# Moving the second pair's K copies, the first V, the weight steps and three squares in an attention and two gated layers

## The chip, the cores and the metric

The kernel runs on one core of a Trainium2 chip. The metric is the device time of one execution in microseconds (us). TensorE (PE) does matrix products and transposes into eight banks of PSUM; VectorE (DVE), ScalarE (ACT) and GpSimd (POOL) do the element work, and GpSimd works on SBUF only; SyncE (SP) issues all transfers. Each engine takes its instructions in the order of the program and waits by semaphores.

## The reference

Three stages, in float32:

```
q_pool = mean of each two rows of q                       (2, 8, 576, 64)
scores = q_pool @ k^T / 8 ; attn = softmax(scores)        (2, 8, 576, 1152)
x = attn @ v, heads side by side                          (1152, 512)
x = rms-normed x * rms_g ; g = x @ w_gate (512 x 1536)
x = (g * sigmoid(g) * (x @ w_val)) @ w_out                (1152, 512)
out = (sigmoid(x @ w_gate2) * (x @ w_val2)) @ w_out2      (1152, 512)
```

The weights come in as words of 64 bits, and the kernel makes float32 of them.

## The kernel before

For precision every operand of a product is split into a high part, rounded to a shorter float, and a low part, the rest; a product is two or three matrix products. The split costs two instructions: one writes the high part (ScalarE, or GpSimd at line 145), one subtracts it (VectorE, or GpSimd at line 146).

**Units of work.** The 16 heads are done in 8 pairs. A pair's scores are 576 query rows in five blocks of 128 rows (`QCOL`; the block c = 0 has half of each head) by three units of 384 keys (`SU`). A *score unit* (`s_unit`, line 476) is two products into one bank (line 505), which VectorE moves out with its maximum (line 509); after three units VectorE reduces the maxima to `nb` (line 511) and ScalarE takes the exponential (line 522). `t_unit` (line 532) transposes the exponentials into a bank (lines 544 and 555) and splits them into `et`: ScalarE writes the high part (line 567) and VectorE the low one (line 568), or ScalarE copies the bank to `er` (line 563) and GpSimd splits it. `av_unit` multiplies with V (line 582). One head takes 18 slots, one transpose unit in each.

**Order.** `at(g, rank, fn)` puts a step into slot g; `run_agenda` calls the steps by slot, then by rank, and each engine gets its instructions in that order. A pair's score units begin 15 slots ahead of its first transposes (`AHEAD`), so the first pair's units are in slots -15 to 19 and the second pair's from slot 21.

**Banks.** PSUM's eight banks have three tags: "s" has two for scores, "t" four for transposes, "o" two for outputs. The first pair's score units use "s" and "o" in turns of two (line 497). The early weight step `w_a1(True)` writes its result to a bank of "t" (line 212).

**Queues.** All transfers are on SyncE's queue, in program order. A transfer that waits holds up all that stand behind it. K, Q and V of a pair are loaded ahead (`load_pair`, `load_v`); a K or Q tile is loaded again only after its reader is through.

**Second pair.** `prep_pair` transposes Q (two groups) and K (three groups) of a pair in the slots `PREP_SECOND`, has GpSimd split them, and then copies the parts on SyncE's queue to where the score products read them: Q in `qq`, K's high part `kh` and low part `kl` into `kk`, in slots `PREP_SECOND_MOVES` (lines 471 to 474). The first score unit of a pair reads the keys 0 to 383, the second 384 to 767. K comes over in a copy of 512 columns and one of 640.

**Weights.** `w_spread` puts five steps of one weight block into the slots `W_SLOTS` of the odd heads 3, 5, 7, 9 and 11: `w_a1` (ScalarE, line 213), `w_b1` and `w_b2` (VectorE, lines 231 and 235), `w_a2` (ScalarE, line 220), `w_b3` (GpSimd, line 241).

**First batch's x.** When the first four pairs are done, `x_steps` takes squares on ScalarE (line 647), roots, norms on GpSimd (line 658) and transposes on TensorE (line 663), in slots counted back from the end of attention, 288 (`X_SQUARES`, `X_TURNS`).

After attention, TensorE does the layers' products (lines 736, 839, 868) while the other engines prepare weights and results.

Of the kernel before, what the change touches and what calls it, by code (L numbers as in the profile page):

```python
# [8 lines left out]
F32 = mybir.dt.float32  # L9
F32R = mybir.dt.float32r  # L10
U32 = mybir.dt.uint32
AF = mybir.ActivationFunctionType
ALU = mybir.AluOpType
# [3 lines left out]
P = 128  # L17
# [15 lines left out]

PREP = (0, 3, 3, 7, 9)
PREP_MOVES = (4, 8, 12, 12)
PREP_SECOND = (3, 6, 7, 11, 12)
PREP_SECOND_MOVES = (11, 12, 14, 14)

PREP_V, POOL_Q, LOAD = 13, 11, 13


FIRST_SUMS, FIRST_Q, SECOND_SUMS, FIRST_V, POOL_Q_SECOND = -1, 3, 4, 7, 11
SECOND_GROUPS = ((6, 3, True, 0), (11, 5, False, 0), (8, 3, True, 1), (11, 3, True, 2), (14, 5, False, 1))
SECOND_DVE = ((False, 1), (True, 0), (True, 2))

W_SLOTS, W_SPLIT = (2, 3, 4, 6, 9), 16
W_WORDS, W_EARLY = 5, 4


X_SQUARES = ((-101, -89, -81), (-54, -59))
X_ROOTS = (-40, -35)
X_NORMS = ((-14, -27, -25), (-20, -17))
X_TURNS = ((-6, -20, -17), (-13, -10))
X_LAST = ((4, 5, 6), (9, 12))

UP_SLOTS = (1, 3, 5, 7)
# [5 lines left out]
def tile_attention_moe_moe(ctx, tc, q, k, v, w_gate1, w_val1, w_out1, rms_g, w_gate2, w_val2, w_out2, out):  # L64
# [3 lines left out]
    nc = tc.nc  # L68
    B, H, S, D = q.shape
# [3 lines left out]
    NK = S // P  # L73
# [21 lines left out]
    def pool(name, side="left", **kw):  # L95
        p = tc.alloc_tile_pool(name=name, bufs=1, side=side, **kw)
        pools.append(p)
        return p
# [9 lines left out]
    ap = pool("ap")  # L108
# [5 lines left out]
    def bank(tag, name):  # L114
        return ps.tile([P, 512], F32, tag=tag, bufs=NBANK[tag], name=name)
# [15 lines left out]
    def at(g, rank, fn):  # L131
        count[0] += 1
        agenda.setdefault(g, []).append((rank, count[0], fn))
# [9 lines left out]
    def split(hi, lo, x):  # L143

        nc.gpsimd.tensor_scalar(hi, x, 1.0, 1.0, op0=ALU.mult, op1=ALU.mult)
        nc.gpsimd.tensor_tensor(lo, x, hi.bitcast(F32), op=ALU.subtract)
# [148 lines left out]
    kk, qq, vv, esb, osb, tbank = {}, {}, {}, {}, {}, {}  # L295
    raw, rcp, xall, sums, both_sums, eneg, oacc, kst = {}, {}, {}, {}, {}, {}, {}, {}
# [20 lines left out]
    def load_v(i):  # L317
        raw["v", i] = ap.tile([P, NK, D], F32, tag="vraw", bufs=1, name="vraw")
        nc.sync.dma_start(raw["v", i], v[i // H, i % H].rearrange("(p c) d -> p c d", c=NK))

    def pool_q(p):
        kr, qr = raw[p]
        qs = ap.tile([P, NQC, P], F32, tag="qsum", bufs=1, name="qsum")
        qd = qs.rearrange("p c (j d) -> p j c d", j=2)
        nc.gpsimd.tensor_tensor(qd, qr[:, :, :, 0:D], qr[:, :, :, D:2 * D], op=ALU.add)
        raw[p] = (kr, qs)

    def prep_v(i):
        vv[i] = ap.tile([P, NK, P], F32R, tag="vv", bufs=2, name="vv")
        split(vv[i][:, :, 0:D], vv[i][:, :, D:P], raw.pop(("v", i)))  # L330
        if i + 1 < NHEAD:
            load_v(i + 1)

    def k_transposes(p, g):
        n = min(4, NK - 4 * g)
        t = bank("t", "kT")
        for c in range(n):
            nc.tensor.transpose(t[:, c * P:(c + 1) * P], raw[p][0][:, 4 * g + c, :], ident)  # L338
        return t[:, 0:n * P], slice(4 * g * P, (4 * g + n) * P)
# [22 lines left out]
    def prep_first():  # L362
# [56 lines left out]
        def head1(g0, is_k, g):  # L419
# [3 lines left out]
            at(g0, 13, lambda: nc.scalar.activation(hi, t, AF.Copy, scale=sc))  # L423
            if (is_k, g) in SECOND_DVE:
                at(g0 + 1, 19, lambda: nc.vector.scalar_tensor_tensor(lo, t, sc, hi.bitcast(F32), op0=ALU.mult, op1=ALU.subtract))
# [25 lines left out]
    def prep_pair(g0, p):  # L451
# [15 lines left out]

        slots, moves = (PREP_SECOND, PREP_SECOND_MOVES) if p == 1 else (PREP, PREP_MOVES)
        for sl, (is_k, g) in zip(slots, ((False, 0), (False, 1), (True, 0), (True, 1), (True, 2))):
# [6 lines left out]
    def s_unit(g, p, k):  # L476

        n, u = divmod(k, NSU)  # L480
        j, c = SCORES[p][n]
        i = 2 * p + j
        both = c == 0 and p > 0
        if k == 0:
            both_sums[p] = ap.tile([P, 2, NQC], F32, tag="sums", bufs=2, name="sums")
            for h in (i, i + 1):
                sums[h] = both_sums[p][:, h - i]
                esb[h] = {}
        if u == 0:
            e = ap.tile([P, NSU * SU], F32, tag="e", bufs=8, name="e")  # L490
            esb[i][c] = e, 0
            if both:
                esb[i + 1][c] = e, 1
            eneg[i, c] = (ap.tile([P, NSU], F32, tag="m", bufs=3, name="m"), ap.tile([P, 1], F32, tag="nb", bufs=3, name="nb"))
        e, _ = esb[i][c]
        m, nb = eneg[i, c]
        s = bank("s" if p or k % 4 < 2 else "o", "s")
        kc = slice(u * SU, (u + 1) * SU)
        if both:
            kh, kl = kst[p]  # L500
            products = ((qbd[:, 0], kh), (qbd[:, 0], kl), (qbd[:, 1], kh))
        else:
            products = [(qq[i][:, part, QCOL[c]:QCOL[c] + P], kk[i]) for part in range(2)]
        for n1, (qs, ks) in enumerate(products):
            nc.tensor.matmul(s[:, 0:SU], qs, ks[:, kc], start=(n1 == 0), stop=(n1 == len(products) - 1))  # L505

        def top():

            nc.vector.tensor_scalar(e[:, kc], s[:, 0:SU], 1.0, None, op0=ALU.mult, op1=ALU.max, accum_out=m[:, u:u + 1])  # L509
            if u == NSU - 1:  # L510
                nc.vector.tensor_reduce(nb, m, op=ALU.max, axis=AX.X, negate=True)

        def swap():
            for h in range(2):
                nc.gpsimd.tensor_copy(sums[i + 1][h * QH:(h + 1) * QH, 0:1], sums[i][(1 - h) * QH:(2 - h) * QH, 0:1])

        def add_small():
            nc.gpsimd.tensor_scalar(both_sums[p], both_sums[p], 1e-9, 1.0, op0=ALU.add, op1=ALU.mult)

        at(g, 17, top)  # L520
        if u == NSU - 1:
            at(g + EXP_LAG, 12, lambda: nc.scalar.activation(e, e, AF.Exp, bias=nb, scale=1.0, accum_out=sums[i][:, c:c + 1]))  # L522
            if both:
                at(g + 4, 24, swap)
            if n == len(SCORES[p]) - 1:
                at(g + 4, 25, add_small)
# [104 lines left out]
    def x_steps(g, b, part):  # L631
# [52 lines left out]
        else:  # L684
            sq = [max(g, END + x) for x in X_SQUARES[part]]
            rt = END + X_ROOTS[part]
            nm = [END + x for x in X_NORMS[part]]
            tt = [END + x for x in X_TURNS[part]]
        for c in range(n):
# [8 lines left out]
    END = NHEAD * NJ  # L698
    S0, S00 = -AHEAD, -AHEAD_FIRST
    prep_first()  # L700
    at(S0 + FIRST_V, 50, lambda: prep_v(0))
    at(S0 + POOL_Q_SECOND, 50, lambda: pool_q(1))
    for p in range(NP):
        for n in range(len(SCORES[p]) * NSU):
            g = 2 * p * NJ + (S0 if p else S00) + n * 2 * NJ // (len(SCORES[p]) * NSU)
            at(g, 2, lambda g=g, p=p, n=n: s_unit(g, p, n))
    for i in range(NHEAD):
        p, odd = divmod(i, 2)
# [205 lines left out]
```

## Time and profile before

| | |
|---|---|
| median of 3 runs | 738.91 us (738.82 to 739.23) |
| profiled execution | 740.92 us, its span 738.7 us |
| TensorE busy | 722.2 us (98% of the span) |
| VectorE, ScalarE, GpSimd busy | 461.0, 432.5, 399.4 us |
| mean granted TensorE clock | 0.993 of full speed |

In rows of a timeline the first number is the start in us from the span's start, the second how long it lasted (of several merged instructions, from the first's start to the last's end); then engine, line, operation, tiles (out<-in), shapes and count; in brackets the idle time of that engine just before and what ended it. "PEld" is TensorE's loading of the operand that stays in the array; it runs beside the products ("PE"), so a pause shows on both with slightly different lengths. "SPq" is SyncE's issuing. A row of the windows view gives a stretch, its length, then the busy us of PE, PEld, DVE, ACT and POOL with their instruction counts, the granted clock (1.00 is 2.4 GHz, 0.50 is 1.2 GHz), the share of the DMA engines that was busy, and GB/s. A row of transfer issues gives out<-in, queue, operation, count, size and the time from issue to landing in us.

### The profile page before, as it was taken

The page shows a single profiled execution, that of the slowest core. Times are in us where ns is not written, and L with a number is a line of the kernel's source. Part 1 is how long each engine was busy: PE and PEld are TensorE (multiplying, and loading weights), DVE is VectorE, ACT ScalarE, POOL GpSimd, SP SyncE. Part 2 cuts the span into 40 slices and gives each one's busy share as a digit, 9 for nine tenths or more (in the row PEclk, how much of TensorE's full clock was granted, in tenths as well). Part 3 has the DMA queues.
Part 4 walks back from the last instruction along what each step waited for, and adds up shares of the span by engine and source line. Part 5 has one row for each costly group of instructions (what it writes and reads, how often), then busy time and mean ns, then how long its engine had stood idle before and what let it go on. Part 6 is the DMA issues. An engine that isn't in the chain of part 4 may idle for free.

```text
span 738.7 us, 12479 instructions
## 1 busy us (share of the span) xinstructions
PE 722.2 (98%) x4501; PEld 692.8 (94%) x4501; DVE 461.0 (62%) x1108; ACT 432.5 (59%) x871; POOL 399.4 (54%) x439
## 2 busy tenths in 40 slices
PE   7969999999999999999999999999999999999997
PEld 6969999999999999999999999999999999998886
DVE  7848988989898887788766754322265455553010
ACT  6748898988899885665544545334255445445000
POOL 5547788888877781466434537443145335437100
PEclk9989999999999999999999999999999999999999
DMA  7443754748365100334223224322032223122011
GB/s 208 103 96 73 175 122 131 163 104 201 74 168 117 46 1 1 115 118 134 89 62 112 87 63 140 92 79 85 29 115 65 78 87 114 58 86 87 0 58 71
DMA packets 69981, 70.30 MB, mean 95 GB/s; under 512 B 19552, under 2 KB 60896, under 8 KB 69920
## 3 DMA queue, kind: packets, MB, share of 16 engines
q1 hardware_dynamic: 69920, 69.51, 33.9%
q8 instruction: 35, 0.57, 0.3%
q14 instruction: 26, 0.21, 0.1%
HBM read 52.69 MB, written 2.36 MB: 75 GB/s over the span
## 4 chain that ended last, share of the span: by engine, by line
PE 93%; DVE 2%; ACT 1%; DMA 1%; SPq 1%; issue 1%; POOL 0%; ACTq 0%; DVEq 0%
PE acc L736 41%; PE s L505 10%; PE acc L839 10%; PE acc L868 10%; PE o L582 10%; PE eT L555 6%; PE eT L544 4%; PE kT L338 1%; PE qT L347 1%; DVE e L509 1%; DVE et L568 1%; DMA kk<-kl 1%; ACT e L522 1%; PE oT L615 1%; PE xT L663 0%
## 5 line engine op out<-in xcount | busy, mean ns | idle before, releaser
L736 PE MATMUL acc<-xh,w 128*128 128x384 f32 (+2 forms) x1184 | 295.8, 331 | 0.0
L736 PEld LDWEIGHTS acc<-xh,w 128*128 128x128 f32 x1184 | 212.0, 188 | 0.0
L736 PE MATMUL acc<-xl,w 128*128 128x384 f32 (+2 forms) x592 | 195.5, 330 | 0.0
L256 POOL TENSOR_TENSOR w<-wr,w 128x512 fp32r<-128x512 f32 x68 | 100.2, 1474 | 160.9 <-ACT w L255 158.5
L509 DVE TENSOR_SCALAR_CACHE_REDUCE e<-s 128x384 f32<-128x384 f32 x219 | 119.3, 551 | 33.0 <-PE s L505 30.4
L582 PE MATMUL o<-et,vv 128*128 128x256 f32 (+1 forms) x576 | 126.2, 327 | 0.2 <-DVE e L509 0.2
L241 POOL TENSOR_TENSOR wr<-wsg,wr 128x512 uint32<-128x512 uint32 x72 | 93.9, 1304 | 44.0 <-DVE wsg L235 44.0
L505 PE MATMUL s<-kk,qq 128*128 128x384 f32 x396 | 108.2, 359 | 9.0 <-DMA kk<-kl 6.2
L736 PEld LDWEIGHTS acc<-xl,w 128*128 128x128 f32 x592 | 111.2, 188 | 0.0
L568 DVE TENSOR_TENSOR et<-eT,et 128x512 fp32r<-128x512 f32 (+1 forms) x173 | 94.7, 554 | 5.4 <-ACT et L567 4.4
L567 ACT ACTIVATE et<-eT 128x512 fp32r<-128x512 f32 (+1 forms) x173 | 83.6, 490 | 23.4 <-PE eT L544 12.1
L747 ACT ACTIVATE sg<-acc 128x384 f32<-128x384 f32 (+2 forms) x74 | 35.4, 481 | 96.1 <-PE acc L736 96.1
L522 ACT ACTIVATE e<-e,nb 128x1152 f32<-128x1152 f32 x73 | 91.3, 1251 | 0.0
L750 DVE TENSOR_TENSOR sg<-acc,sg 128x384 f32<-128x384 f32 (+2 forms) x74 | 40.5, 547 | 80.2 <-PE acc L736 74.4
L582 PEld LDWEIGHTS o<-et,vv 128*128 128x128 f32 x576 | 82.9, 192 | 0.7 <-DVE e L509 0.5
L213 ACT ACTIVATE wg<-wraw 128x512 f32<-128x512 f32 x72 | 48.2, 669 | 52.9 <-DVE wsg L235 32.2
L235 DVE SCALAR_TENSOR_TENSOR wsg<-wg,wsg 128x512 uint32<-128x512 uint32 x72 | 77.1, 1071 | 2.3
L505 PEld LDWEIGHTS s<-kk,qq 128*128 128x128 f32 x396 | 63.6, 192 | 11.8 <-issue 6.4
L839 PE MATMUL acc<-hh,w 128*128 128x384 f32 x288 | 73.3, 334 | 0.0
L231 DVE TENSOR_SCALAR wsg<-wg 128x512 uint32<-128x512 uint32 x72 | 42.6, 592 | 35.1 <-POOL wr L241 35.0
L555 PE MATMUL eT<-ident,e 128*128 128x128 f32 x351 | 61.9, 276 | 1.3 <-ACT er L563 0.6
L544 PE MATMUL eT<-ident,e 128*128 128x128 f32 x288 | 54.0, 275 | 0.0
(113 smaller groups left out, 1085.3 us busy)
## 6 DMA issues: line engine op xcount, KB each, us to landing
wraw<-in_moe_w_gate_dram SPq DMA_DIRECT2D x24, 512.0 KB, 3.5
wraw<-in_moe_w_val_dram SPq DMA_DIRECT2D x24, 512.0 KB, 3.5
wraw<-in_moe_w_out_dram SPq DMA_DIRECT2D x24, 512.0 KB, 3.4
qq<-qq SPq DMA_DIRECT2D x21, 288.0 KB, 3.2
vraw<-in_v_dram SPq DMA_DIRECT2D x16, 288.0 KB, 3.7
kraw<-in_k_dram SPq DMA_DIRECT2D x14, 288.0 KB, 5.1
qraw<-in_q_dram SPq DMA_DIRECT2D x14, 256.0 KB, 4.5
out_dram<-ob SPq DMA_DIRECT2D x9, 256.0 KB, 2.0
```

Source lines behind the costliest of these rows:

```text
L241: nc.gpsimd.tensor_tensor(x["r"], x["s"], x["r"], op=ALU.add)
L256: nc.gpsimd.tensor_tensor(t[:, 1], r, t[:, 0].bitcast(F32), op=ALU.subtract)
L505: nc.tensor.matmul(s[:, 0:SU], qs, ks[:, kc], start=(n1 == 0), stop=(n1 == len(products) - 1))
L509: nc.vector.tensor_scalar(e[:, kc], s[:, 0:SU], 1.0, None, op0=ALU.mult, op1=ALU.max, accum_out=m[:, u:u + 1])
L522: at(g + EXP_LAG, 12, lambda: nc.scalar.activation(e, e, AF.Exp, bias=nb, scale=1.0, accum_out=sums[i][:, c:c + 1]))
L544: nc.tensor.transpose(t[:, o:o + P], esb[i][c][0][:, ks], ident)
L555: nc.tensor.transpose(t[:, o:o + P], e[:, ks], ident if c or half else swap_id)
L567: at(g, 12, lambda: nc.scalar.activation(hi, t, AF.Copy))
L568: at(g + 1, 20, lambda: nc.vector.tensor_tensor(lo, t, hi.bitcast(F32), op=ALU.subtract))
L582: nc.tensor.matmul(o[:, 0:n], vv[i][:, kc, :], et[:, k, x * n:(x + 1) * n], start=(done == 0), stop=(done == 2 * NK - 1))
L736: nc.tensor.matmul(acc[:, 0:nt], wt[:, ws, dc * P:(dc + 1) * P], xs[:, dc], start=(dc == 0 and n == 0), stop=(dc == NDM - 1 and n == 2))
L839: nc.tensor.matmul(acc[t][:, 0:NTT], w[:, ws, (fc % 4) * P:(fc % 4 + 1) * P], hs[fc][:, cs], start=(fc == 0 and n == 0), stop=(fc == NFC - ...
```

## The change

- The second pair's last two K transposes come in slots 10 and 11 (11 and 12 before); Q's copies in slot 10, K's copies in 11, 12 and 12 (12, 14 and 14 before), so ahead of slot 13, where the next V and the third pair are loaded.
- The first V is split in two steps: its high half in slot 10 of the start, its low half in slot 12 (slots counted from -15), where both came in slot 7; the sum of the second pair's Q comes in slot 12 instead of 11.
- The low part of the second head's first K group is made on GpSimd, with a copy by ScalarE, instead of on VectorE.
- The first pair's score units from slot 0 on use only the banks "s".
- The weight steps come in the slots 4, 5, 6, 8, 10 of their heads.
- Two of the first batch's three early squares move from slots 187 and 199 to 210 and 214 (the third stays at 207); two x transposes move one slot later.

```diff
-PREP_SECOND = (3, 6, 7, 11, 12)
-PREP_SECOND_MOVES = (11, 12, 14, 14)
+PREP_SECOND = (3, 6, 7, 10, 11)
+PREP_SECOND_MOVES = (10, 11, 12, 12)
-FIRST_SUMS, FIRST_Q, SECOND_SUMS, FIRST_V, POOL_Q_SECOND = -1, 3, 4, 7, 11
+FIRST_SUMS, FIRST_Q, SECOND_SUMS, FIRST_V, POOL_Q_SECOND = -1, 3, 4, (10, 12), 12
-SECOND_DVE = ((False, 1), (True, 0), (True, 2))
+SECOND_DVE = ((False, 1), (True, 2))
-W_SLOTS, W_SPLIT = (2, 3, 4, 6, 9), 16
+W_SLOTS, W_SPLIT = (4, 5, 6, 8, 10), 16
-X_SQUARES = ((-101, -89, -81), (-54, -59))
+X_SQUARES = ((-78, -74, -81), (-54, -59))
-X_TURNS = ((-6, -20, -17), (-13, -10))
+X_TURNS = ((-6, -20, -17), (-12, -9))
...
+    def first_v(lower):
+        if not lower:
+            vv[0] = ap.tile([P, NK, P], F32R, tag="vv", bufs=2, name="vv")
+            nc.gpsimd.tensor_scalar(vv[0][:, :, 0:D], raw["v", 0], 1.0, 1.0, op0=ALU.mult, op1=ALU.mult)
+            return
+        nc.gpsimd.tensor_tensor(vv[0][:, :, D:P], raw.pop(("v", 0)), vv[0][:, :, 0:D].bitcast(F32), op=ALU.subtract)
+        load_v(1)
...
-        s = bank("s" if p or k % 4 < 2 else "o", "s")
+        s = bank("s" if p or g >= 0 or k % 4 < 2 else "o", "s")
...
-    at(S0 + FIRST_V, 50, lambda: prep_v(0))
-    at(S0 + POOL_Q_SECOND, 50, lambda: pool_q(1))
+    for sl, lower in zip(FIRST_V, (False, True)):
+        at(S0 + sl, 52, lambda lower=lower: first_v(lower))
+    at(S0 + POOL_Q_SECOND, 51, lambda: pool_q(1))
```

What the change does to the order shows at three places. On SyncE's queue, at the second pair's copies (`qq`, `kk` from `kh` and `kl`) and the loads (`vraw`, `qraw`, `kraw`), before:

```order
L358 DMA qq<-qq 64x1152 x3
L358 DMA kk<-kh 64x512
L358 DMA kk<-kl 64x512
L319 DMA vraw<-in_v_dram 128x576
L308 DMA qraw<-in_q_dram 128x4x128 x2
L311 DMA qraw<-in_q_dram 64x2x128 x2
L314 DMA kraw<-in_k_dram 128x9x64 x2
L358 DMA kk<-kh 64x640
L358 DMA kk<-kl 64x640
L358 DMA kk<-kh 64x1152
L358 DMA kk<-kl 64x1152
```

The same place now (the lines are ten further on):

```order
L367 DMA qq<-qq 64x1152 x3
L367 DMA kk<-kh 64x512
L367 DMA kk<-kl 64x512
L367 DMA kk<-kh 64x640
L367 DMA kk<-kl 64x640
L367 DMA kk<-kh 64x1152
L367 DMA kk<-kl 64x1152
L320 DMA vraw<-in_v_dram 128x576
L309 DMA qraw<-in_q_dram 128x4x128 x2
L312 DMA qraw<-in_q_dram 64x2x128 x2
L315 DMA kraw<-in_k_dram 128x9x64 x2
```

Four copies went from behind the seven loads to a place ahead of them.

On GpSimd, in the start (`qsum` from `first`: the second head's Q sum; `kk` and `qq` from `kqt`: low parts of the second head; `vv`: the first V; `qsum` from `qraw`: the second pair's Q sum), before:

```order
L400 TENSOR_TENSOR qsum<-first 128x5x64 x2
L145 TENSOR_SCALAR vv<-vraw 128x9x64
L146 TENSOR_TENSOR vv<-vraw,vv 128x9x64
L429 TENSOR_TENSOR kk<-kqt,kk 64x384
L325 TENSOR_TENSOR qsum<-qraw 128x2x5x64
L429 TENSOR_TENSOR qq<-kqt,qq 128x320
```

And now:

```order
L409 TENSOR_TENSOR qsum<-first 128x5x64 x2
L438 TENSOR_TENSOR kk<-kqt,kk 64x384 x2
L338 TENSOR_SCALAR vv<-vraw 128x9x64
L438 TENSOR_TENSOR qq<-kqt,qq 128x320
L326 TENSOR_TENSOR qsum<-qraw 128x2x5x64
L340 TENSOR_TENSOR vv<-vraw,vv 128x9x64
```

One more low part of K came in, Q's low part went ahead of the Q sum, and V's lower half went behind it.

On VectorE, in an odd head with weight steps (`e,m<-s`: a score unit moved out; `et<-eT`: a low part of transposed exponentials; `wsg`: the weight steps), before:

```order
L592 TENSOR_TENSOR osb<-o,osb 64x256
L231 TENSOR_SCALAR wsg<-wg 128x512
L509 TENSOR_SCALAR e,m<-s 128x384
L568 TENSOR_TENSOR et<-eT,et 128x320
L235 SCALAR_TENSOR_TENSOR wsg<-wg,wsg 128x512
L509 TENSOR_SCALAR e,m<-s 128x384
L511 TENSOR_REDUCE nb<-m 128x1
L568 TENSOR_TENSOR et<-eT,et 128x320
L509 TENSOR_SCALAR e,m<-s 128x384 x2
```

And now:

```order
L601 TENSOR_TENSOR osb<-o,osb 64x256
L518 TENSOR_SCALAR e,m<-s 128x384
L577 TENSOR_TENSOR et<-eT,et 128x320
L518 TENSOR_SCALAR e,m<-s 128x384
L520 TENSOR_REDUCE nb<-m 128x1
L232 TENSOR_SCALAR wsg<-wg 128x512
L577 TENSOR_TENSOR et<-eT,et 128x320
L236 SCALAR_TENSOR_TENSOR wsg<-wg,wsg 128x512
L518 TENSOR_SCALAR e,m<-s 128x384 x2
```

The two weight steps went behind the second of the score units, on both sides of an `et`.

## Rows read from the trace of the kernel before

**Rows 1.** Page, part 1: busy us, share of the span, instructions

```profile
PE 722.2 (98%) x4501; PEld 692.8 (94%) x4501; DVE 461.0 (62%) x1108; ACT 432.5 (59%) x871; POOL 399.4 (54%) x439
```

**Rows 2.** Timeline of PE at the second pair's second score unit

```profile
43.94 0.98 PE L505 MATMUL s<-kk,qq 128*128 128x384 f32 x2 [6.18 <-DMA kk<-kl]
```

**Rows 3.** Timeline of SyncE's queue, 20 to 46 us

```profile
...
30.16 0.73 SPq L358 DMA_DIRECT2D kk<-kl  x1
...
39.28 0.59 SPq L358 DMA_DIRECT2D kk<-kl  x1
...
```

**Rows 4.** Transfer issues, 20 to 50 us: size and time to landing

```profile
...
kk<-kl SPq DMA_DIRECT2D x1, 160.0 KB, 4.5
...
kk<-kl SPq DMA_DIRECT2D x1, 128.0 KB, 3.1
...
```

**Rows 5.** Timeline of POOL: low parts of the second pair's Q and K

```profile
23.56 0.74 POOL L146 TENSOR_TENSOR qq<-kqt,qq 128x256 fp32r<-128x256 f32 x1
...
30.71 0.46 POOL L146 TENSOR_TENSOR kl<-kqt,kh 128x128 fp32r<-128x128 f32 x1
```

**Rows 6.** Windows: three stretches of the first 50 us

```profile
0.00:9.70 9.70, 7.34 (x34) 5.33 (x35) 4.97 (x16) 4.48 (x7) 4.48 (x15) 1.00 0.51 149
...
18.80:22.00 3.20, 3.20 (x15) 3.01 (x14) 1.96 (x9) 2.07 (x4) 1.91 (x4) 0.50 0.02 5
...
43.90:49.20 5.30, 5.26 (x21) 5.06 (x22) 2.18 (x7) 1.31 (x3) 1.55 (x4) 0.50 0.09 24
```

**Rows 7.** Timeline of all engines, 12 to 34 us

```profile
15.33 0.55 DVE L509 TENSOR_SCALAR_CACHE_REDUCE e<-s 128x384 f32<-128x384 f32 x1
...
17.02 0.59 ACT L567 ACTIVATE et<-eT 128x512 fp32r<-128x512 f32 x1
...
17.45 0.19 PEld L505 LDWEIGHTS s<-kk,qq 128*128 128x128 f32 x1 [1.99 <-POOL qq L429]
...
17.65 0.69 DVE L568 TENSOR_TENSOR et<-eT,et 128x512 fp32r<-128x512 f32 x1 [0.29 <-ACT et L567]
...
18.75 0.55 PEld L505 LDWEIGHTS s<-kk,qq 128*128 128x128 f32 x2
...
22.47 0.30 PEld L505 LDWEIGHTS s<-kk,qq 128*128 128x128 f32 x2 [0.28 <-DVE e L509]
...
29.12 0.30 PEld L582 LDWEIGHTS o<-et,vv 128*128 128x128 f32 x2 [0.46 <-DVE e L509]
...
33.26 0.30 PEld L505 LDWEIGHTS s<-kk,qq 128*128 128x128 f32 x2 [0.30 <-DVE e L509]
```

**Rows 8.** Timeline, 142 to 149 us: an odd head with weight steps

```profile
142.27 0.65 ACT L213 ACTIVATE wg<-wraw 128x512 f32<-128x512 f32 x1
...
143.95 0.69 DVE L231 TENSOR_SCALAR wsg<-wg 128x512 uint32<-128x512 uint32 x1
...
144.82 0.43 ACT L563 ACTIVATE er<-eT 128x320 f32<-128x320 f32 x1
...
145.29 0.31 PEld L555 LDWEIGHTS eT<-ident,e 128*128 128x128 f32 x3 [0.41 <-ACT er L563]
...
146.70 0.48 DVE L568 TENSOR_TENSOR et<-eT,et 128x320 fp32r<-128x320 f32 x1
...
147.10 0.55 DVE L509 TENSOR_SCALAR_CACHE_REDUCE e<-s 128x384 f32<-128x384 f32 x1
...
147.78 0.34 PEld L505 LDWEIGHTS s<-kk,qq 128*128 128x128 f32 x2
```

**Rows 9.** Timeline of PEld, 160 to 214 us: its waits

```profile
177.59 0.31 PEld L555 LDWEIGHTS eT<-ident,e 128*128 128x128 f32 x3 [0.41 <-ACT er L563]
...
202.84 0.30 PEld L505 LDWEIGHTS s<-kk,qq 128*128 128x128 f32 x2 [0.82 <-DVE e L509]
210.99 0.31 PEld L555 LDWEIGHTS eT<-ident,e 128*128 128x128 f32 x3 [0.82 <-ACT er L563]
```

**Rows 10.** Timeline of PEld, 268 to 276 us: a wait of the x transposes

```profile
274.02 0.42 PEld L663 LDWEIGHTS xT<-ident,x 128*128 128x128 f32 x4 [0.40 <-POOL x L658]
```

## The prediction

> **What bounds the kernel now.** I read the page's busy shares first. TensorE is busy 722.2 of 738.7 us [rows 1], so only its pauses and its slow clock can be saved, some 16 us of pauses in all. The timeline of TensorE then shows where the largest pause is: at 43.94 a score unit starts after 6.18 us in which TensorE waited for a copy of K's low part into kk, so it had arrived at 37.76 [rows 2]. The view of SyncE's queue says why that copy is late: the copies of the first 512 columns are issued up to 30.16 + 0.73 = 30.9, but the low part of the last 640 columns only at 39.28 [rows 3]. In between stand the loads of the next V and of the third pair, and the first of those waits for GpSimd's work on V. From its issue the copy takes 4.5 us to land [rows 4], 39.28 + 4.5 = 43.8. The two parts of K that it copies had been ready since 30.71 + 0.46 = 31.2 [rows 5]. So this is a place in a queue, not a shortage.
>
> The windows view shows a second price of pauses. After the wait the granted clock stands at 0.50 (1.2 GHz) from 43.9 to 49.2 with TensorE busy 5.26 of 5.30 us; the same happens from 18.8 to 22.0 [rows 6], after the pause that ends at 17.45 [rows 7]. In the first 9.7 us, where TensorE also pauses 2.4 us in small pieces, the clock stays at 1.00 [rows 6].
>
> **The copies of K (slots 12 and 14 become 11 and 12).** Removed: the seven load issues that stood ahead. In the changed queue the two copies of the last 640 columns stand straight behind those of the first 512. On the old clock they would be issued at 30.9 and about 31.5 (0.59 each [rows 3]) and land at 31.5 + 4.5 = 36.0; with the 3.1 us that the 128 KB copies took [rows 4] it would be 34.6. TensorE wants them at 37.76. Both sides start sooner in the new kernel, as the next parts show. TensorE comes 2.6 us sooner. The copies hang on Q's low part, ready at 23.56 + 0.74 = 24.3 [rows 5], which gains only the part before it, about 1.9 us (1.6 and 0.28 below). So the copies land at about 34.1 and TensorE asks at 35.1: a margin of 1.0 us, and of 2.4 with the shorter landing. Their data is no limit: the last two K transposes come a slot sooner on TensorE, so GpSimd's 31.2 moves by the 1.9 and about a slot more, to about 28.5, before SyncE is there at 31.5 - 1.9 = 29.6. The whole 6.2 goes. Bounds: 6.2 at best; if the landing took 3 us more, 2 us of the wait would stay. The loads behind are later by the four copies' issue time, 4 x 0.6 = 2.4 us; the third pair's Q and K are not used until the next head, over 10 us on, and that is their cover.
>
> The slow clock after the wait goes with it: 5.26 us at half speed are 2.6 us of work, so 2.6 come back. The other engines could refuse that speed; in that window VectorE was busy 2.18 and ScalarE 1.31 of 5.30 us [rows 6], which doubled are 82% and 49%. So I take the whole; the low bound is 0.
>
> **The start, slots -9 to 5.** GpSimd now makes two low parts of K's heads in place of one, puts Q's low part ahead of the Q sum and V's lower half behind it. The 1.99 us wait of TensorE for Q's low part at 17.45 [rows 7] goes, since this part no longer stands behind both V instructions and the Q sum. But two things hold TensorE instead. First, from slot 0 on all score units (counted from 0; unit 13 is the first) use the two banks "s", where units 14, 15, 18, 19, 22, 23, 26 and 27 had "o". Unit 14 now waits until VectorE has moved unit 12 out: 15.33 + 0.55 = 15.9 [rows 7], some 0.3 sooner because VectorE has one K part less; before, it didn't wait. Second, unit 17 waits for unit 15 to be moved out. On VectorE that stands behind the subtraction for et, which starts at 17.65 because ScalarE only comes to et at 17.02, behind two exponentials that the change doesn't touch [rows 7]. So unit 17 starts at 17.65 + 0.69 + 0.55 = 18.9, and before it started at 18.75 [rows 7]. I book 0 up to here (bounds: 0.4 lost, 0.7 gained). V's halves cost nothing: the first product with V comes after unit 17, and GpSimd is through by then. Should that cover fail, it is one such instruction, by the 0.74 us that 256 columns took [rows 5] 0.74 x 576/256 = 1.7 us.
>
> What does change is the shape of the pause: in place of 2 us in one piece there are about 1.2 (before unit 14) and 0.9 (before unit 17), with work between. The small pauses of the first 9.7 us left the clock alone, so I take it that these do too, and the 3.2 us at half speed give 1.6 back; the low bound is 0. The three waits at 22.47, 29.12 and 33.26 for banks that scores and outputs had shared, 0.28 + 0.46 + 0.30 = 1.0 [rows 7], go as well, because VectorE no longer starts the stretch behind; low bound again 0.
>
> **A rule against this.** Perfetto Trace Analysis (section Matmul Optimizations) in the Trainium skill asks that all eight PSUM banks be used so that more instructions can overlap; the change takes two from the scores. The waits above show TensorE stopped by either arrangement. By the rule more waits come than go; that is the last rival below.
>
> **Weight steps (slots 2, 3, 4, 6, 9 become 4, 5, 6, 8, 10), five odd heads.** Before, the first step on ScalarE (0.65 at 142.27) holds a transpose bank, and the transposes at 145.29 wait 0.41 for the bank that er at 144.82 gives back [rows 8]. Now the step comes later, these transposes get another bank, and the 0.41 goes. But ScalarE does the step after that er: 144.82 + 0.43 = 145.25, plus 0.65 = 145.9. VectorE works without a gap from its first weight step at 143.95 to 147.10, 3.15 us [rows 8]; starts follow each other about 0.08 closer than the durations add up, so 1.2 of it are the two weight steps (0.69 the first, the second alike) and 0.4 the et at 146.70, and both weight steps and this et now stand at the end. So it reaches the first one at 143.95 + 3.15 - 1.6 = 145.5, idles 0.4, and what it did at 147.10 it does at 147.5. This is the move that frees the bank of the unit at 147.78 [rows 8], now 147.5 + 0.55 = 148.05. TensorE is late by 0.27 a head, 5 x 0.27 = 1.4 lost. Bounds: 5 x 0.41 = 2.0 gained if VectorE's idle time is absorbed, 5 x 0.65 = 3.3 lost.
>
> **Squares and turns.** The wait of 145.29 returns at 177.59, 32.30 us on, and then at 210.99, 33.40 on [rows 8, 9]: that pair is 1.1 longer, with a wait of 0.82 at 202.84 and one of 0.82 in place of 0.41. Two squares on ScalarE are the only addition there. They move to slots 12 and 16 of the odd head, where ScalarE has gaps: 1.1 gained (bounds 0 and 1.1). The x transposes one slot later pass the 0.40 wait for GpSimd's norm at 274.02 [rows 10]: 0.4 (bounds 0 and 0.6).
>
> **Sum.** -6.2 - 2.6 - 1.6 - 1.0 - 1.1 - 0.4 + 1.4 = -11.5. The layers after attention are bound by TensorE and keep this. The profiled execution took 740.92 us (its span 738.7 and 2.2 around it), so 729.4; the median of the runs is 2.0 lower, so 727.4.
>
> **Rivals.**
> - The clock falls at the start as before (the pauses add up to nearly the same 2 us): 1.6 less gain, 729.0. For it: the pause only splits. Against: the work between. 14%.
> - The copies still come late, because they meet each other and Q's third copy in the DMA engines: with 3 us more in landing, 2 us of waiting stay, and a pause of that size cost the clock at 17.45, another 1.6: 731.0; with 5 us more, 733. The 1.0 margin speaks for it, the shorter landing against. 12%.
> - The weight steps pay: -2.0 in place of +1.4, 724.0. 10%.
> - Nothing is won, because the wait for kk only shows another reason (the data, a later copy): 738 to 739. 31.2 against 39.28 speaks against it. 3%.
> - Slower: two banks for the scores. If each unit from slot 0 on waits as unit 17 does, the pauses hold the clock at 0.50 until the copies' place. From 18.8 to 37.76 TensorE did some 19 - 1.6 - 1.0 = 16 us of full-speed work, which at half speed is 32: it comes to that place at 51 in place of 43.9 (wait included), 7 later, less the 2.6 of the slow clock behind it: 743. It decides at about half the units waiting 0.9. Against it: from the second pair on the scores run in these two banks, and TensorE's only large wait for them is at 202.84. 3%.
> - As forecast, the terms within a microsecond or two: 58%.
>
> A measurement of this kernel can tell 0.2%, 1.5 us, from no change. Faster by more than that: all but the last two and what fails together with them, 0.93; the same 0.04; slower 0.03. The forecast's own range is 725.5 to 729.5; to hold 8 in 10 it takes in the clock and part of the late copies above, and the weight steps' gain below: 724.0 to 732.0.
>
> **What would show it.** Right: no wait of TensorE for kk, or one under 0.3 us; the granted clock at 1.00 from 15 to 50 us; SyncE issuing all six K copies in a row by about 31; unit 17 at 18.5 to 19; the five waits for er gone and five new waits of scores for VectorE; the pairs 32.3 to 32.7 apart, the last no longer 33.4. Wrong: a row of 0.50 in the start; a wait for kk of over 1 us; waits of score units for VectorE all through the first 35 us.

## The result, and the profile after

The changed kernel takes 729.46 us (median of 4 runs, 729.38 to 729.59), the kernel before 738.87 in the same comparison (4 runs, 738.41 to 739.23). The ratio is 0.9873, 95% interval 0.9856 to 0.9890: faster by 9.4 us. The forecast was 727.4 in a range of 724.0 to 732.0, so the direction and the range held and the gain was put 2.1 too large. The profiled execution took 729.40 us; its span is 727.6, so 1.8 lie around it. Line numbers of the changed kernel are one to ten higher than before (the copies L358 are now L367, the loads L319 now L320).

Part 1 of the page of the changed kernel, to be held against [rows 1]: TensorE does the same 4501 matmuls in 3.7 us less busy time, for the most part because the two stretches at half speed of [rows 6] are gone; the other 7.4 us of the shorter span are pauses that are gone.

```profile
PE 718.5 (99%) x4501; PEld 689.3 (95%) x4501; DVE 459.3 (63%) x1107; ACT 432.8 (59%) x872; POOL 400.3 (55%) x440
```

SyncE's queue in the changed kernel, 27 to 34 us (start, duration, line, transfer). All six copies of K now stand in a row and the load of V behind them; the last is issued up to 31.40 + 0.78 = 32.2 (by about 31 was forecast).

```profile
27.91 0.54 SPq L367 DMA_DIRECT2D kk<-kh  x1
...
30.06 0.55 SPq L367 DMA_DIRECT2D kk<-kl  x1
30.66 0.69 SPq L367 DMA_DIRECT2D kk<-kh  x1
31.40 0.78 SPq L367 DMA_DIRECT2D kk<-kl  x1
32.22 1.32 SPq L320 DMA_DIRECT2D vraw<-in_v_dram  x1
```

The transfer issues of the same stretch: the low part that TensorE waited for before takes 3.6 us to land, so it is there at 30.06 + 3.6 = 33.7.

```profile
kk<-kl SPq DMA_DIRECT2D x1, 160.0 KB, 3.6
```

TensorE's timeline at the place of [rows 2]: the second pair's second unit, without a wait. It starts at 35.08 (35.1 was forecast), 1.4 after the landing (a margin of 1.0 was forecast).

```profile
35.08 0.60 PE L514 MATMUL s<-kk,qq 128*128 128x384 f32 x2
```

The windows view of the changed kernel, columns as in [rows 6]: the clock stays at 1.00 through the start and through the stretch in which the pause stood.

```profile
15.00:18.80 3.80, 2.58 (x18) 2.24 (x18) 3.24 (x13) 3.80 (x9) 3.52 (x4) 1.00 0.58 195
18.80:22.00 3.20, 3.20 (x25) 3.10 (x26) 3.08 (x10) 2.26 (x6) 1.93 (x6) 1.00 0.33 100
36.00:44.00 8.00, 8.00 (x59) 7.73 (x58) 6.58 (x22) 6.59 (x13) 6.75 (x10) 1.00 0.67 174
```

TensorE's weight loads of the changed kernel, 12 to 24 us and 120 to 150 us. The first two rows are the pauses before units 14 and 17, where the two banks "s" are full; they are the two that the prediction named, in the place of the one pause and the three later waits of [rows 7], and none of the three is left. The third is one of the five new waits in the odd heads with weight steps, in the place of the five waits for er of [rows 8].

```profile
15.58 0.30 PEld L514 LDWEIGHTS s<-kk,qq 128*128 128x128 f32 x2 [1.50 <-DVE e L518]
...
18.75 0.30 PEld L514 LDWEIGHTS s<-kk,qq 128*128 128x128 f32 x2 [0.88 <-DVE e L518]
...
137.32 0.30 PEld L514 LDWEIGHTS s<-kk,qq 128*128 128x128 f32 x2 [0.51 <-DVE e L518]
```

VectorE in that head. The two weight steps (wsg) stand ahead of the move that frees the unit's bank, which ends at 136.71 + 0.55 = 137.26; the unit starts at 137.32.

```profile
135.11 0.69 DVE L232 TENSOR_SCALAR wsg<-wg 128x512 uint32<-128x512 uint32 x1 [0.28 <-ACT wg L214]
135.72 0.48 DVE L577 TENSOR_TENSOR et<-eT,et 128x320 fp32r<-128x320 f32 x1
136.11 0.68 DVE L236 SCALAR_TENSOR_TENSOR wsg<-wg,wsg 128x512 uint32<-128x512 uint32 x1
136.71 0.55 DVE L518 TENSOR_SCALAR_CACHE_REDUCE e<-s 128x384 f32<-128x384 f32 x1
```

### The profile page after: what moved, and what is told of

Its sections match the earlier page's. It is cut to its first block, busy times and chain, and to the rows that moved or that the text cites. A ratio compares the mean times of both kernels' runs of the same rounds, so it can differ in the third digit from the quotient of the medians.

```text
span 727.6 us, 12508 instructions
## 1 busy us (share of the span) xinstructions
PE 718.5 (99%) x4501; PEld 689.3 (95%) x4501; DVE 459.3 (63%) x1107; ACT 432.8 (59%) x872; POOL 400.3 (55%) x440
## 4 chain that ended last, share of the span: by engine, by line
PE 93%; DVE 3%; ACT 2%; issue 1%; DMA 0%; POOL 0%; ACTq 0%; DVEq 0%
PE acc L746 41%; PE acc L849 10%; PE acc L878 10%; PE s L514 10%; PE o L591 9%; PE eT L564 5%; PE eT L553 4%; PE kT L347 1%; ACT e L531 1%; DVE e L518 1%; PE qT L356 1%; PE oT L624 1%; DVE et L577 1%; PE xT L672 0%; DVE wsg L232 0%
## 5 line engine op out<-in xcount | busy, mean ns | idle before, releaser
L214 ACT ACTIVATE wg<-wraw 128x512 f32<-128x512 f32 x72 | 48.2, 670 | 52.9 <-DVE wsg L236 32.2
L564 PE MATMUL eT<-ident,e 128*128 128x128 f32 x351 | 61.0, 273 | 0.2 <-DVE et L577 0.2
L221 ACT ACTIVATE wr<-wraw 128x512 uint32<-128x512 uint32 x72 | 47.9, 666 | 9.8 <-POOL w L257 9.0
```

The lines of the kernel that those rows point to most:

```text
L564: nc.tensor.transpose(t[:, o:o + P], e[:, ks], ident if c or half else swap_id)
```

## The experiments

All are timed against the kernel before, which stood at 739.65, 739.54 and 739.15 (medians) in the three comparisons. Times of variants of the changed kernel are compared with its 729.46. The runs of a kernel without the wait for kk lie within 0.4 us from lowest to highest. The changed kernel was not timed again beside its variants, so a difference of 0.3 to 0.5 us is taken as real only where the traces show it at its place too (differences of the spans, or of the place where a stretch begins).

**The kernel before once more.** No edit.

> The kernel before, unchanged, once more, to see whether its profiled execution (740.92, 2.0 above its median) stands for its other ones. Theory: it does not; in most executions TensorE loses less at half clock, so the runs are at 738.4 to 739.3 with a mean granted clock above 0.993, and a new profile shows either the 0.50 stretch at 18.8 to 22.0 or the one at 43.9 to 49.2 shorter by about 2 us of work. Rival: the same stretches at 0.50 and the same pauses as in the first profile, and about 741 for the profiled execution: then profiling costs this kernel 2 us that it does not cost the changed one.

Measured 739.58 (11 runs, 737.87 to 741.29). The new profiled execution took 739.33. Its windows show 1.00 in the start, where the first profile had 0.50, and the half-speed stretch after the pause only until about 47.4 (the third row shows it up to 47.1):

```profile
15.00:18.80 3.80, 2.56 (x17) 2.02 (x16) 3.72 (x15) 3.46 (x9) 2.22 (x2) 1.00 0.98 290
18.80:22.00 3.20, 2.60 (x20) 2.27 (x19) 2.99 (x12) 2.20 (x5) 2.52 (x6) 1.00 0.02 5
42.80:47.10 4.30, 4.30 (x18) 4.07 (x18) 2.00 (x7) 0.88 (x2) 1.53 (x3) 0.50 0.09 22
```

Its weight loads show what [rows 7] had under a slow clock, now at full speed: the wait for Q's low part, and three bank waits of which the first is 0.83 in place of 0.28.

```profile
17.27 0.19 PEld L505 LDWEIGHTS s<-kk,qq 128*128 128x128 f32 x1 [1.46 <-POOL qq L429]
21.26 0.30 PEld L505 LDWEIGHTS s<-kk,qq 128*128 128x128 f32 x2 [0.83 <-DVE e L509]
27.89 0.30 PEld L582 LDWEIGHTS o<-et,vv 128*128 128x128 f32 x2 [0.46 <-DVE e L509]
32.04 0.30 PEld L505 LDWEIGHTS s<-kk,qq 128*128 128x128 f32 x2 [0.30 <-DVE e L509]
```

So the theory holds for the profile, though not for its range of times (738.4 to 739.3 was forecast). Both profiled times lie within the spread of the other executions, so a cost of profiling itself isn't shown. Of 55 executions of the kernel before in the three comparisons, 9 had its mean granted clock of 0.993 and took 740.14 to 741.57; 46 had 0.995 or 0.997 and took 737.87 to 740.37; the median of all is 739.48. How many of them had half speed in the start isn't on record: 0.993 comes up too in the two variants below that have the changed start and the wait for kk. The two profiled executions differ by 740.92 - 739.33 = 1.6, and the traces show where: the unit behind the wait for kk starts at 43.94 in the first and 42.79 in this one, 1.15 apart (0.16 already at unit 17, then 1.6 of slow clock less the 0.55 by which the first bank wait is longer here); another 0.4 is the stretch behind the wait, with about 5.5 us at half speed in the first and 4.6 here.

**Only the copies.** In the kernel before:

```diff
-PREP_SECOND = (3, 6, 7, 11, 12)
-PREP_SECOND_MOVES = (11, 12, 14, 14)
+PREP_SECOND = (3, 6, 7, 10, 11)
+PREP_SECOND_MOVES = (10, 11, 12, 12)
```

> The kernel before with only K's parts and copies of the second pair moved (slots 11, 12 to 10, 11; copies 11, 12, 14, 14 to 10, 11, 12, 12). Theory, by the prediction's terms: 6.2 of waiting and up to 2.6 of slow clock behind it go, 730.1 (6.2 alone: 732.7), with no wait of TensorE for kk above 0.3. Rival: without the earlier start on VectorE and GpSimd the copies' data comes too late, a wait of 1 to 2 us stays and the time is 732 to 734.

Measured 730.93 (730.81 to 731.04), 8.7 under the 739.65 of the same comparison. No wait for kk is left, and the mean clock is 1.00; the first transposes of an output (oT) start at 47.29, in the second profile of the kernel before at 55.59, 8.3 later. TensorE's timelines of the second profile, of this run and of the changed kernel at that place:

```profile
55.59 0.49 PE L615 MATMUL oT<-ident,osb 128*128 128x128 f32 x3
47.29 0.49 PE L615 MATMUL oT<-ident,osb 128*128 128x128 f32 x3
45.73 0.49 PE L624 MATMUL oT<-ident,osb 128*128 128x128 f32 x3
```

So 6.2 of waiting and 2.1 to 2.5 of slow clock went, nearly as the prediction's first two terms had it, without the start's other edits.

**The copies and K's parts put back** in the changed kernel (the same two lines the other way).

> The changed kernel with these slots put back to the old ones. Theory: the wait for kk returns at 6 us or a little more, since TensorE comes 2.6 sooner and the copy's place behind the loads of V is set by GpSimd, and the clock falls behind it: 729.5 + 6.2 + 2.6 = 738.3, or 735.7 without the clock. Rival: the start's other edits had already pulled the copies forward, and the time is under 733.

Measured 738.21 (737.29 to 739.36); the wait is back and a little longer:

```profile
42.18 0.98 PE L514 MATMUL s<-kk,qq 128*128 128x384 f32 x2 [6.61 <-DMA kk<-kl]
```

**Only the last two copies put back**, behind the loads:

```diff
-PREP_SECOND_MOVES = (10, 11, 12, 12)
+PREP_SECOND_MOVES = (10, 11, 14, 14)
```

> The changed kernel with only the two copies of the last 640 columns put back into slot 14, behind the loads; K's transposes and parts stay in their new slots. Theory (a place in SyncE's queue, not data): the wait for kk returns as with both put back, 6 to 7, the granted clock falls behind it, and the time is 737.5 to 739. Rival: the earlier parts of K matter too, and it is 1 us or more below the 738.2 of the run with both put back.

Measured 737.10 (736.42 to 738.69), 0.4 below the theory's range. Most of the gain hangs on these two places in the queue alone, 737.10 - 729.46 = 7.6. The rival may have a part: with K's parts in their new slots the median is 1.1 below that of the run with both put back, and the wait in the profile is 5.84 in place of 6.61. That isn't shown for sure, since the runs of either kernel spread over 2 us, and as ratios to the kernel before, 0.9975 and 0.9984, they are 0.7 apart. In the windows of this run the clock is at 0.50 before TensorE goes on at 41.29, falling while the engine stands still:

```profile
36.00:38.00 2.00, 0.00 (x0) 0.00 (x0) 0.48 (x1) 1.22 (x2) 0.78 (x1) 1.00 1.04 232
38.00:40.00 2.00, 0.00 (x0) 0.00 (x0) 0.00 (x0) 0.00 (x0) 0.00 (x0) 0.84 1.08 241
40.00:42.00 2.00, 0.71 (x2) 0.71 (x3) 0.00 (x0) 0.00 (x0) 0.00 (x0) 0.50 0.81 181
```

**The old start** in the changed kernel: V in one piece, three low parts on VectorE, Q's low part at slot 11, and the old banks.

```diff
-FIRST_SUMS, FIRST_Q, SECOND_SUMS, FIRST_V, POOL_Q_SECOND = -1, 3, 4, (10, 12), 12
+FIRST_SUMS, FIRST_Q, SECOND_SUMS, FIRST_V, POOL_Q_SECOND = -1, 3, 4, 7, 11
-SECOND_DVE = ((False, 1), (True, 2))
+SECOND_DVE = ((False, 1), (True, 0), (True, 2))
...
-    for sl, lower in zip(FIRST_V, (False, True)):
-        at(S0 + sl, 52, lambda lower=lower: first_v(lower))
+    at(S0 + FIRST_V, 50, lambda: prep_v(0))
...
-        s = bank("s" if p or g >= 0 or k % 4 < 2 else "o", "s")
+        s = bank("s" if p or k % 4 < 2 else "o", "s")
```

> The changed kernel with the start as before: V in one piece at slot 7, three low parts on VectorE, Q's low part at slot 11, the units from slot 0 on in the banks s and o by turns. Theory: the one pause of 2 us comes back, the clock falls to 0.50 behind it for some 3 us (1.6) and the three bank waits return (1.0): 729.5 + 2.6 = 732.1. Rival 1: the clock does not fall and the waits are absorbed: 729.5 to 730.5. Rival 2: later data for K's copies adds a wait for kk of 1 us or more: over 733.

Measured 730.80 (730.64 to 730.98): 1.3 slower. The theory's clock term is refuted: the granted clock is 1.00 from 15 to 22 us with the pause of 1.64 back. The bank waits come back whole (0.75, 0.57 and 0.30), so rival 1 has the clock right and the waits wrong; no wait for kk comes. The weight load behind the pause, and the windows:

```profile
17.51 0.19 PEld L514 LDWEIGHTS s<-kk,qq 128*128 128x128 f32 x1 [1.64 <-POOL qq L438]
15.00:18.80 3.80, 2.38 (x17) 1.80 (x16) 3.70 (x14) 3.30 (x8) 2.38 (x3) 1.00 0.93 281
18.80:22.00 3.20, 2.69 (x21) 2.35 (x20) 3.06 (x11) 2.44 (x6) 2.32 (x5) 1.00 0.05 17
```

**The old banks alone**, all else new (the last line of that diff).

> The changed kernel with the first pair's score units in the banks s and o by turns again, all else new. Theory: the pauses before units 14 and 17 (1.50 and 0.88 on the weight loads) go, and waits for the banks shared with the outputs come back later, 0.83, 0.46 and 0.30 as in the kernel before; the sums are nearly equal and the time is 728.7 to 729.7. Rival 1: the shared banks cost more than the pauses, over 730. Rival 2: nothing stands in for the pauses, 728.0.

Measured 730.74 (730.72 to 730.76): rival 1. The weight loads show why the two arrangements are not equal: the unit at 21.14 needs an "o" bank that VectorE empties late, and the transposes at 16.80 come to Q's sum before GpSimd is through with it.

```profile
16.80 0.31 PEld L356 LDWEIGHTS qT<-ident,qsum 128*128 128x128 f32 x3 [1.08 <-POOL qsum L326]
21.14 0.30 PEld L514 LDWEIGHTS s<-kk,qq 128*128 128x128 f32 x2 [1.57 <-DVE e L518]
```

So the bank line is worth the whole 1.3 of the start, and the halves of V, the low parts and Q's slot give nothing without it (730.74 against 730.80). What the bank line would give without them was not tried.

**Units 14 and 15 alone in "o".**

```diff
-        s = bank("s" if p or g >= 0 or k % 4 < 2 else "o", "s")
+        s = bank("s" if p or g >= 4 or k % 4 < 2 else "o", "s")
```

> The changed kernel with units 14 and 15 alone put into the banks o, which no output needs before 19.3, and all later units in s. Theory: both pauses go, unit 14 and unit 17 start without a wait, no shared bank is waited for later, and the time falls by 1.0 to 2.0 to 727.5 to 728.5. Rival: what TensorE does next, the products for et of ScalarE at 17 and the outputs at 19.3, holds it at the same place, and the time stays at 729.5.

Measured 729.08 (728.93 to 729.31), 0.4 faster and short of the theory; in the traces the first transposes of an output come 0.31 sooner (45.42 against 45.73). Its weight loads show the successors, Q's sum on GpSimd and then VectorE again:

```profile
16.77 0.31 PEld L356 LDWEIGHTS qT<-ident,qsum 128*128 128x128 f32 x3 [1.09 <-POOL qsum L326]
19.20 0.30 PEld L514 LDWEIGHTS s<-kk,qq 128*128 128x128 f32 x2 [0.47 <-DVE e L518]
20.28 0.30 PEld L514 LDWEIGHTS s<-kk,qq 128*128 128x128 f32 x2 [0.26 <-DVE e L518]
```

**The old weight slots.**

```diff
-W_SLOTS, W_SPLIT = (4, 5, 6, 8, 10), 16
+W_SLOTS, W_SPLIT = (2, 3, 4, 6, 9), 16
```

> The changed kernel with the weight steps back in slots 2, 3, 4, 6, 9. Theory, by the prediction's term: the five new waits of a score unit for VectorE (0.51 each) give way to the five old ones for er (0.41 each, and the work behind them), the pairs stand 32.30 apart in place of 32.57, and the time falls by 5 x 0.27 = 1.4 to 728.1. Rival: the moved slots are worth something elsewhere, for instance the pair with the squares, and the time is 729.5 or more.

Measured 728.36 (728.30 to 728.67), 1.1 faster. The waits for er are back, five of 0.40 to 0.41, one of them here:

```profile
133.84 0.31 PEld L564 LDWEIGHTS eT<-ident,e 128*128 128x128 f32 x3 [0.41 <-ACT er L572]
```

The pairs stand 32.27 apart in place of 32.57. TensorE's timelines, the first transposes of an output two pairs apart, in this run (207.06 - 142.52 = 64.54) and in the changed kernel (65.13):

```profile
142.52 0.49 PE L624 MATMUL oT<-ident,osb 128*128 128x128 f32 x3
207.06 0.49 PE L624 MATMUL oT<-ident,osb 128*128 128x128 f32 x3
143.48 0.49 PE L624 MATMUL oT<-ident,osb 128*128 128x128 f32 x3
208.61 0.49 PE L624 MATMUL oT<-ident,osb 128*128 128x128 f32 x3
```

Five pairs make 1.5, which is the difference of the spans (727.6 - 726.1); 0.4 of it is lost again around the span, 2.2 in place of 1.8.

**The old squares.**

```diff
-X_SQUARES = ((-78, -74, -81), (-54, -59))
+X_SQUARES = ((-101, -89, -81), (-54, -59))
```

> The changed kernel with the squares back at -101 and -89 of the end. Theory: the pair in which they stand is 1.0 to 1.1 longer again, with waits of TensorE for a score bank on VectorE or for er on ScalarE, 730.5. Rival: with the new weight steps these squares fall into other gaps and cost nothing, 729.5.

Measured 729.98 (729.81 to 730.07), 0.5 slower (0.6 in the span), between theory and rival; the pair is 33.23 long in place of 32.57. One wait is back, and the er wait that had doubled at 210.99 in [rows 9] is not, since the new weight slots have removed its kind:

```profile
192.62 0.30 PEld L514 LDWEIGHTS s<-kk,qq 128*128 128x128 f32 x2 [0.82 <-DVE e L518]
```

**Three combinations**, each with units 14 and 15 in "o": the old weight slots; the second step on VectorE a slot later (first diff); and the first step's result in SBUF in place of a transpose bank, with its readers later (second diff).

```diff
-W_SLOTS, W_SPLIT = (4, 5, 6, 8, 10), 16
+W_SLOTS, W_SPLIT = (4, 5, 7, 8, 10), 16
```

```diff
-W_SLOTS, W_SPLIT = (4, 5, 6, 8, 10), 16
+W_SLOTS, W_SPLIT = (4, 6, 8, 9, 10), 16
-                for sl, step in zip(W_SLOTS, (lambda: w_a1(True), w_b1, w_b2, w_a2, w_b3)):
+                for sl, step in zip(W_SLOTS, (lambda: w_a1(False), w_b1, w_b2, w_a2, w_b3)):
```

> Two single edits together: weight steps in their old slots, and units 14 and 15 alone in the banks o. They act in different stretches (five odd heads; before 22 us), so theory: 728.36 - 0.38 = 728.0. Rival: they share a cause and the time stays at 728.4.

Measured 728.08 (727.99 to 728.13): the two single gains add up, to within 0.1.

> Weight steps in slots 4, 5, 7, 8, 10 (the second step on VectorE behind the score unit's move in place of ahead of it), and units 14 and 15 alone in o. Theory: the unit that waited 0.51 for VectorE finds its bank 0.6 sooner, no wait of TensorE stays in these heads, the pairs stand 32.1 to 32.2 apart in place of 32.57, and the time is 729.08 - 5 x 0.4 = 727.1. Rival: the bank that the first weight step holds until the second has read it is then missed by a group of transposes, 0.4 to 0.6 a head: 729 or more.

Measured 727.54 (727.47 to 727.66). The wait of 0.51 is gone and the pairs are 32.18 apart, 0.4 less than with the change, as forecast; the time is 0.4 above the forecast. In its trace the first transposes of an output come 0.35 later than with units 14 and 15 alone (45.77 against 45.42), and most of that is there at 9.91 (9.58 with units 14 and 15 alone), behind a load of the first K, where the edit changes nothing.

> Weight steps in slots 4, 6, 8, 9, 10 with the first step's result in SBUF in place of a transpose bank, and units 14 and 15 alone in o. Theory: no transpose waits for a bank held by the weight steps and no score unit for VectorE: pairs 32.1 to 32.2 apart, 727.1. Rival: VectorE takes longer to read it from SBUF, or the steps at 8 to 10 delay the next head's first moves, and the wait comes back 1 to 2 us later: 728.5 to 729.5.

Measured 727.30 (727.16 to 727.43), the fastest of all, 2.2 under the changed kernel (ratio to the kernel before 0.9842, 0.9829 to 0.9856). The pairs are 32.06 apart, and in some heads 0.15 of the wait for VectorE is left. The slots and the place of the result were changed together, so what either gives isn't told apart. The rival's longer read is half true: with its input in SBUF the first step takes 0.46 in place of 0.69, the second 0.83 in place of 0.68.

```profile
134.66 0.46 DVE L232 TENSOR_SCALAR wsg<-wg 128x512 uint32<-128x512 uint32 x1
...
136.40 0.83 DVE L236 SCALAR_TENSOR_TENSOR wsg<-wg,wsg 128x512 uint32<-128x512 uint32 x1
```

## Why the prediction was right, and where it missed

**Copies of K, -6.2 and -2.6: right.** Alone they gave 8.7 of the 8.8. The reading that it was a place in a queue holds, 7.6 of it with the data left early. The rival of late copies was wrong: the landing took 3.6, and the margin was 1.4.

**Slow clock in the start, -1.6, and the step to the median, -2.0: the step that failed.** The sum was made against an execution of 740.92 and gave 729.4 for it; the changed kernel's profiled execution took 729.40. The mistake was "the median of the runs is 2.0 lower, so 727.4". Of those 2.0, 1.6 is what a second profile doesn't have, for the most part the slow stretch at the start (1.15, net of a longer bank wait). The sum had already taken that out as a gain, so it was taken off twice. The rows [rows 6] showed the stretch; that it was the reason for the 2.0 I didn't ask. The other 0.4 lies within what a median of three runs can miss by: 738.91, where 55 executions have 739.48.

The mechanism behind the -1.6 isn't borne out either. The prediction had the clock fall after one pause of 2 us and stay up because the pause was split. But with the pause in one piece it stayed at 1.00 in three traces: 1.46 us in the second profile of the kernel before, 1.68 with only the copies moved, 1.64 with the old start. So the 1.00 that was to show the forecast right came, and no run shows that the change brought it about. Nor is 729.4 against 729.40 a proof of the sum: the span shrank by 11.1, 0.4 less than the 11.5, and the time around the span by 0.4 (2.2 to 1.8), which no term had. That they cancel is luck.

**The start's waits, -1.0: mis-sized, in the same knot.** Where the clock doesn't fall, the three bank waits are 0.83 + 0.46 + 0.30 = 1.6; a TensorE at half speed comes later to the first of them and finds 0.28. In the traces the first transposes of an output start at 57.13 in the first profile of the kernel before, at 55.59 in the second, and at 45.73 in the changed one: 11.4 against the first (6.2 + 2.6 + 1.6 + 1.0), and 9.9 against the second (6.2 + 2.3 + 1.6 would be 10.1). The 0 booked up to unit 17 was right within its bounds: 18.75 in the first profile, 18.59 in the second, 18.75 now.

**Weight steps, +1.4: right in the span.** A pair is 0.27 to 0.30 longer, as worked out: 32.57 against 32.30 in [rows 8, 9] and 32.27 with the old slots. Five pairs make 1.5; the time gives back 0.4 of it around the span, so the steps cost 1.1.

**Squares, -1.1, and turns, -0.4.** Two squares moved, the third stayed. Their pair went from 33.40 to 32.57, and since the weight steps add 0.27 to 0.30 there, the squares gave the 1.1 that was forecast, beside the new weight slots. But the two edits share a wait, the one for er that had doubled, so that the squares alone are worth 0.5 (0.6 in the span) once the weight steps have moved. Of the turns only 0.1 came, so this term was mis-sized. The wait of 0.40 for the norm is gone [rows 10], but a new one of 0.18 for VectorE's et stands at 262.98, and one that was 0.22 before is 0.26. I had named no successor there. TensorE's weight loads, the last row of the kernel before and the first two of the changed one:

```profile
262.98 0.19 PEld L591 LDWEIGHTS o<-et,vv 128*128 128x128 f32 x1 [0.18 <-DVE et L577]
269.62 0.20 PEld L553 LDWEIGHTS eT<-ident,e 128*128 128x128 f32 x2 [0.26 <-DVE et L577]
280.71 0.20 PEld L544 LDWEIGHTS eT<-ident,e 128*128 128x128 f32 x2 [0.22 <-DVE et L568]
```

Against the second profile of the kernel before the balance is: copies 8.3, start 1.6, squares 1.1, turns 0.1, less 1.5 for the weight steps, 9.6, where the spans differ by 9.5 (737.1 - 727.6); with the 0.4 around them the times differ by 9.9, 739.33 - 729.40.

**The rivals.** None of the five came. The first, with the clock falling at the start, has the nearest number, 729.0, but its mechanism didn't occur. The slower one, two banks for the scores holding the clock low, is refuted by 1.00 in all windows of the start. The rule weighed there, Perfetto Trace Analysis in the Trainium skill (section Matmul Optimizations), asks for all eight PSUM banks to be used. Both kernels use all eight; the change only ends, from slot 0 on, a sharing of the two output banks with the scores, so the rule as a whole wasn't tested. The runs show that this sharing costs 1.3 (730.74 against 729.46); only for the two units that come before any output does it pay, 0.4 (729.08).

## What to carry to other kernels

Where an engine waits for a DMA, look first at when it was issued and what stood ahead of it in its queue; the data had been ready 8 us before. Before a profiled execution is turned into a forecast for the median, find what makes it longer than the median: if a term of the sum is that very thing, it must not be subtracted again. A wait removed upstream at full clock uncovers the next one, so each removed wait needs its successor named.

## What the runs showed of the hardware

Kernels that keep the 6 us pause of TensorE spread over 2.1 to 3.7 us from run to run (737.29 to 739.36 and 736.42 to 738.69 for the changed kernel with copies put back, 737.87 to 741.57 for 55 executions of the kernel before), with mean clocks from 0.993 to 0.997; without it they spread over 0.04 to 0.4 us at 0.999 to 1.00. The same program, with a pause of 1.99 us in one trace and of 1.46 in the other, fell to 1.2 GHz at the start in one execution and stayed at 2.4 in the other. What decides it isn't settled here.

The time around the span is 1.8 us in every kernel with the weight steps in the changed slots or later ones, and 2.1 to 2.2 with them in the old slots, in all runs. No run here tells why.
